# Loading rows of keys and rearranging the opening of an attention + two-MLP kernel

## The chip, the cores and the metric

The kernel runs on one NeuronCore of a Trainium2 chip. The metric is device time in microseconds (us), from launch to end. The kernel before takes 1071.01 us (median of three runs, 1069.24 to 1071.11). Its engines have one instruction queue each: PE (TensorE, the matmuls; PEld is its weight load), DVE (VectorE), ACT (ScalarE), POOL (GpSimd), and SP, which here only issues DMAs. An instruction waits at the head of its queue for semaphores, and everything behind it waits with it.

## The reference

Chunked attention over 4 batches, 8 heads, 768 positions of width 64: each chunk of 32 queries sees 8 memory keys and a window of the sequence. Two MLPs of width 512 to 2048 to 512 follow, over 3072 tokens.

```python
for c in range(nc):                      # 24 chunks of 32 queries
    l_start, r_end = max(0, c*32 - 16), min(S, c*32 + 32 + 8)
    k_full = concat([mem_k, k[:, :, l_start:r_end]])      # 8 + up to 56 keys
    scores = scale * q_c @ k_full.T
    a = exp(scores - max(scores)); a = a / (sum(a) + 1e-9)
    out[chunk] = a @ concat([mem_v, v[:, :, l_start:r_end]])
x = out as 3072 x 512
h = x @ w_in;  x = (h - tanh(h)) @ w_out                  # first MLP
h = x @ w2_in; x = g2(h) @ w2_out                         # second MLP, g2 = clipped (h+1)^2/4
```

The weights come as 64-bit words. The kernel reads them as pairs of 32-bit integers and turns each pair into a float by a few integer operations ("rounding" below).

## The kernel before, in words

**Attention by groups.** Four chunks (128 queries, all heads) make a group; there are 24 groups, and four groups make a block of 512 tokens. For one group `att_scores` runs 64 small matmuls (64x32 by 64x64) into PSUM, `att_max` takes the maxima and subtracts them (DVE), `att_exp` is one ACT instruction, `att_sum` adds and inverts (DVE), `att_transpose` turns the weights by four PE matmuls against an identity, `att_at` copies them out (ACT), `att_values` runs 64 small matmuls, `att_norm` divides (DVE), `att_x` transposes the result (PE), `att_xh` and `att_xl` write it as a rounded part (ACT) and a rest (DVE): `xh`, `xl`, the input of the first MLP.

**The input.** The host lays out, for each chunk, its queries, 128 keys (`KEYS`: 8 of memory and 120 of the sequence, for each of four head pairs) and the values. A chunk needs only the first 64 of these keys (`WIN`): the memory and 56 of the sequence. Before, each chunk's 64 keys are a DMA of their own, 128 partitions by four runs of 64 floats (`att_keys`, line 364).

**The opening** is what the change touches: the first four groups, with a queue order written by hand (no scheduler moves anything). Their loads are issued on SP group by group: queries, four key windows, a weight slice `w_in` (from the second group on), four loads of values; then the fourth weight slice. Then come the loads of group 4, and the weight slices 4, 5, 6 and 7, each into one of four `stage` buffers, which is free when the POOL addition of the slice before in it is done. While the groups run, PE is given extra matmuls on zeros (`warm`, `fill`). Before, each of groups 0 to 2 has ten of them, in three places.

**Weight slices.** Slice i is rounded in five instructions after its load: two on ACT (`round_act`, lines 138 and 141), two on DVE (`round_mag`, 147 and 148), one on DVE (`round_sign`, 156) and an integer addition on POOL (161). Then ACT makes its rounded part `whi` (173) and DVE the rest `wlo` (180). The first MLP's first product, `hidden(s)`, takes slice s: `whi` by `xh`, `whi` by `xl`, `wlo` by `xh`, four matmuls each, into a PSUM tile `h`; then `gate` applies tanh and the subtraction. Its first step, `hidden(0)`, is run early for the 384 tokens of groups 0 to 2, in between the work of group 3, and for the last 128 tokens after group 3.

After the opening the kernel interleaves the `hidden` and `output` products of the first MLP with the attention of the later groups, then runs the second MLP, up to the end at about 1070 us.

Of the kernel before, what the change touches and what calls it, by code (L numbers as in the profile page):

```python
# [8 lines left out]
F32 = mybir.dt.float32  # L9
# [18 lines left out]
KEYS = NMEM + CTX  # L28
WIN = NMEM + LEFT + CHUNK + SEEN
NPAIR = H // 2  # L30
KC = DM // 128
FC = DFF // 128
NEG = -3.0e38

GC = 4
# [7 lines left out]


WARM = 11
KEEP = {"s": 6, "t": 2, "v": 2}

LAG = FC

# [29 lines left out]
def tile_memory_attention_two_mlps(  # L79
# [25 lines left out]
    def slot(tag, name, dtype=F32):  # L105
        return slots.tile([128, 512], dtype, tag=tag, name=name)
# [13 lines left out]
    def load_weights(phase, which, fc, tag=None):  # L120
        src = ((w1_in, w1_out), (w2_in, w2_out))[phase][which]
        if tag is None:
            tag = f"stage{loaded[0] % STAGES}"
            loaded[0] += 1
        stage = wide.tile([128, 512, 2], I32, tag=tag, name=f"stage{phase}{which}_{fc}")
        nc.sync.dma_start(out=stage, in_=src[fc])
        stage_t[phase, which, fc] = stage
# [25 lines left out]
    def round_sign(phase, which, fc):  # L153
        stage = stage_t.pop((phase, which, fc))
        bits = raw_t[phase, which, fc].bitcast(I32)
        nc.vector.scalar_tensor_tensor(
            out=bits, in0=stage[:, :, 1], scalar=-0x40000000, in1=bits, op0=ALU.bitwise_and, op1=ALU.bitwise_or
        )

        eng = nc.vector if phase else nc.gpsimd  # L160
        eng.tensor_tensor(out=bits, in0=bits, in1=stage[:, :, 0], op=ALU.add)  # L161
# [14 lines left out]
    def split_weights_lo(s, which):  # L176
        phase, b, fc = steps[s]
        r, hi = raw_t[phase, which, fc], split_t[s, which]
        lo = slot(f"wlo{which}_{s % (W1O if which else 2)}", f"wlo{which}_{s}", F32R)
        nc.vector.tensor_tensor(out=lo, in0=r, in1=hi.bitcast(F32), op=ALU.subtract)  # L180
        split_t[s, which] = hi, lo
# [162 lines left out]
    def att_load_start(t, values):  # L344
        if not free:
            free.extend(slot(f"g{i}", f"start{i}") for i in range(FC))
            free.extend(slot(f"y{i}", f"starty{i}") for i in range(KC))
        q, k0, k1, v0, v1 = free[5 * t:5 * t + 5]
        if values:
            att_v(t, (v0, v1))  # L350
        else:
            att_keys(t, q, (k0, k1))

    def att_keys(t, q, k):
        q = q.rearrange("p (j a c) -> p j a c", j=GC, a=NPAIR)
        k = [x.rearrange("p (j a c) -> p j a c", j=2, a=NPAIR) for x in k]
        src = qkv[t * GC:(t + 1) * GC]
        nc.sync.dma_start(
            out=q.rearrange("p j a c -> p j (a c)"),
            in_=src[:, :, :NPAIR * TQ].rearrange("j p c -> p j c"),  # L360
        )
        ks = src[:, :, NPAIR * TQ:QK].rearrange("j p (a c) -> j p a c", a=NPAIR)
        for j in range(GC):
            nc.sync.dma_start(out=k[j // 2][:, j % 2], in_=ks[j, :, :, :WIN])  # L364
        st[t] = {
            "q": [q[:, j] for j in range(GC)],
            "k": [k[j // 2][:, j % 2] for j in range(GC)],
        }

    def att_v(t, v):  # L370
        v = [x.rearrange("p (j c) -> p j c", j=2) for x in v]
        src = qkv[t * GC:(t + 1) * GC]

        for i in range(2):
            for u in range(2):
                c = QK + u * 4 * D
                nc.sync.dma_start(
                    out=v[i][u * WIN:(u + 1) * WIN],
                    in_=src[2 * i:2 * i + 2, :WIN, c:c + 4 * D].rearrange("j p c -> p j c"),
                )  # L380
        st[t]["v"] = [v[j // 2][:, j % 2] for j in range(GC)]
# [5 lines left out]
    def att_scores(t, pair):  # L387
        qt, kt = st[t]["q"], st[t]["k"]
        sp = pair[:, :, 4 * D:].rearrange("p c (a k) -> p c a k", a=NPAIR)
        for pr in range(NPAIR):  # L390
            for j in range(GC):
                for hh in range(2):
                    nc.tensor.matmul(  # L393
                        sp[j * CHUNK:(j + 1) * CHUNK, hh, pr, :],
                        qt[j][hh * D:(hh + 1) * D, pr, :],
                        kt[j][hh * D:(hh + 1) * D, pr, :],
                        start=True, stop=True,
                    )
        st[t]["sp"] = sp

    def att_max(t):

        e = slots.tile([128, 4, 2, WIN], F32, tag=f"e{t % 2}", name=f"e{t}")
        mx = att.tile([128, 2, NPAIR], F32, tag="mx", name=f"mx{t}")
        s = st[t]["sp"]

        if t % GPB == 0:
            nc.vector.memset(s[:CHUNK, :, :, NMEM:NMEM + LEFT], NEG)
        if t % GPB == GPB - 1:
            nc.vector.memset(s[128 - CHUNK:, :, :, WIN - SEEN:], NEG)  # L410
        nc.vector.tensor_reduce(out=mx, in_=s, op=ALU.max, axis=AX.X)
        st[t]["e"] = e
        if t in BY_HEAD:
            nc.vector.tensor_scalar(out=mx, in0=mx, scalar1=-scale, scalar2=None, op0=ALU.mult)
            st[t]["mx"] = mx
            return
        for hh in range(2):
            nc.vector.tensor_tensor(
                out=e.rearrange("p (b c) u k -> p c u b k", c=2)[:, hh],
                in0=s[:, hh].rearrange("p (u b) k -> p u b k", u=2),  # L420
                in1=mx[:, hh].rearrange("p (u b) -> p u b", u=2)[:, :, :, None].to_broadcast([128, 2, 2, WIN]),
                op=ALU.subtract,
            )
# [71 lines left out]
    def att_xl(t):  # L495
        b, o = t // PER, t % PER * GQ
        xh, xl = x_tiles(0, b)
        nc.vector.tensor_tensor(  # L498
            out=xl[:, :, o:o + GQ], in0=st.pop(t)["xp"], in1=xh[:, :, o:o + GQ].bitcast(F32), op=ALU.subtract
        )  # L500
# [52 lines left out]
    def hidden(s, n0=0, n1=N, parts=range(3)):  # L553
        phase, b, fc = steps[s]
        xh, xl = x_tiles(phase, b)
        hi, lo = split_t[s, 0]
        if s not in h_t:
            h_t[s] = ps_h.tile([128, 512], F32, tag="h", name=f"h{s}")[:, :N]
        hp = h_t[s][:, n0:n1]
        for j in parts:  # L560
            w, x = ((hi, xh), (hi, xl), (lo, xh))[j]
            for kc in range(KC):
                nc.tensor.matmul(  # L563
                    hp, w[:, kc * 128:(kc + 1) * 128], x[:, kc, n0:n1],
                    start=j == 0 and kc == 0, stop=j == 2 and kc == KC - 1,
                )
# [471 lines left out]
    def warm(n, ps):  # L1038
        for _ in range(n):
            nc.tensor.matmul(ps, zeros[:, :128], zeros, start=True, stop=True)  # L1040
# [3 lines left out]
    warm(WARM, fill)  # L1044
    for j in range(PER):
        att_load_start(j, False)
        if j:
            load_weights(0, 0, j - 1)
        att_load_start(j, True)
    load_weights(0, 0, PER - 1)  # L1050
    att_load(PER)

    def start_scores(j):
        pool, tag = ((ps_a, "a"), (ps_acc, "acc0"))[j % 2]
        st_pair[j] = pool.tile([128, 2, 512], F32, tag=tag, name=f"start_a{j}")
        att_scores(j, st_pair[j])

    start_scores(0)
    for j in range(PER):
        last = j == PER - 1  # L1060
        if not last:
            warm(KEEP["s"], fill)
        att_max(j)
        if j:
            att_xl(j - 1)
        if last:
            split_weights_lo(0, 0)
            hidden(0, 0, EARLY_N, (0,))
        if 1 < j:
            round_sign(0, 0, j - 2)  # L1070
        att_exp(j)
        att_sum(j)
        tx = ps_acc.tile([128, 2, 512], F32, tag="acc1", name=f"start_tx{j}")
        att_transpose(j, tx[:, 0, :])
        att_at(j)
        if j == 2:
            split_weights_hi(0, 0)
        if j:
            round_act(0, 0, j - 1)
        if last:  # L1080
            split_weights_hi(1, 0)
            hidden(0, 0, EARLY_N, (1,))
        else:
            warm(KEEP["t"], fill)
        att_values(j, st_pair.pop(j))
        if last:
            hidden(0, 0, EARLY_N, (2,))
        else:
            warm(KEEP["v"], fill)
            start_scores(j + 1)  # L1090
        att_norm(j)
        if last:
            split_weights_lo(1, 0)
        if j:
            round_mag(0, 0, j - 1)
        att_x(j, tx[:, 1, :])
        att_xh(j)
    att_xl(PER - 1)
    round_sign(0, 0, 2)
    round_act(0, 0, 3)  # L1100
    round_rest(0, 0, 3)
    for j in range(AHEAD):
# [105 lines left out]
```

## Time and profile before

| | |
|---|---|
| runs | 1071.01, 1071.11, 1069.24 us |
| profiled execution: span, first to last instruction | 1070.1 us |
| what lies around the span (median of the runs less the span) | 0.9 us |
| PE busy | 1052.4 us (98%), 7589 matmuls |
| DVE, ACT, POOL busy | 855.7, 650.0, 42.7 us |
| bytes by DMA | 259.37 MB, mean 242 GB/s |
| chain that ended last, by engine | PE 93%, DMA 2%, SP queue 2%, ACT 1%, DVE 1% |

The share of PE says little by itself: in the opening it counts the matmuls on zeros. So the stages have to be read apart: the first 55 us, in which PE stops and waits, and the rest, in which it hardly does. In the rows of the trace, the time at a row's start is counted from the span's start, and the bracket at its end says how long the engine had stood idle before it and what ended that.

### The profile page before, as it was taken

How to read it: one execution, taken by the hardware profiler on the slowest of the kernel's cores; microseconds unless marked ns; L12 is line 12 of the kernel's file. 1: busy time of each engine (PE TensorE's matmuls, PEld its weight loads, DVE VectorE, ACT ScalarE, POOL GpSimd, SP SyncE). 2: the span in 40 equal slices, each digit the busy share in tenths (PEclk: the TensorE clock that was granted, in tenths of full speed). 3: DMA queues.
4: the chain of work that ended last, by engine and by line, in shares of the span. 5: the costliest groups of instructions: out<-in, count | busy, mean ns of one | idle time of the engine just before them, and what ended most of it. 6: DMA issues, size and time to landing. Idle time of an engine off the chain costs nothing.

```text
span 1070.1 us, 21112 instructions
## 1 busy us (share of the span) xinstructions
PE 1052.4 (98%) x7589; PEld 859.7 (80%) x7589; DVE 855.7 (80%) x1511; ACT 650.0 (61%) x1203; POOL 42.7 (4%) x38
## 2 busy tenths in 40 slices
PE   7799999999999999999999999999999999999998
PEld 3577888888888888888888888888888888888887
DVE  4898987877799999999999778698477787476854
ACT  2687756555455565565566677757477666577553
POOL 0232212000000000000000000000000000000000
PEclk9999999999999999999999999999999999999999
DMA  8999887898889999876487978787766877766774
GB/s 207 245 258 247 260 240 207 258 292 272 266 269 315 325 302 292 292 261 205 154 278 263 313 221 259 210 277 214 232 194 195 261 224 232 214 194 195 203 203 146
DMA packets 212088, 259.37 MB, mean 242 GB/s; under 512 B 65424, under 2 KB 129168, under 8 KB 211984
## 3 DMA queue, kind: packets, MB, share of 16 engines
q1 hardware_dynamic: 211840, 257.88, 80.2%
q8 instruction: 61, 1.00, 0.4%
q14 instruction: 43, 0.35, 0.1%
q10 hardware_dynamic: 144, 0.13, 0.0%
HBM read 199.23 MB, written 58.72 MB: 241 GB/s over the span
## 4 chain that ended last, share of the span: by engine, by line
PE 93%; DMA 2%; SPq 2%; ACT 1%; DVE 1%; issue 0%; ACTq 0%
PE h L563 23%; PE acc L893 21%; PE acc L601 17%; PE qa L805 12%; PE qc L805 6%; PE qb L805 3%; PE acc_-1_1_7132 L893 2%; PE acc_-1_0_7131 L893 2%; DMA stage<-w_in 2%; PE a L467 1%; SPq L364 1%; PE a L393 1%; PE acc_-1_1_7508 L893 1%; PE acc_-1_0_7507 L893 1%; PE b L487 1%; PE b L453 1%
## 5 line engine op out<-in xcount | busy, mean ns | idle before, releaser
L893 PE MATMUL acc<-ghi,inG 128*128 128x512 f32 x672 | 183.0, 389 | 0.0
L576 ACT ACTIVATE g<-h 128x512 f32<-128x512 f32 x96 | 57.7, 601 | 176.7 <-PE h L563 154.9
L893 PEld LDWEIGHTS acc<-ghi,inG 128*128 128x128 f32 x672 | 126.2, 188 | 26.1
L227 DVE TENSOR_TENSOR glo<-g,ghi 128x512 fp32r<-128x512 f32 x174 | 117.8, 688 | 27.4 <-ACT ghi L226 26.3
L805 PE MATMUL qa<-xc,inP 128*128 128x512 f32 x576 | 139.3, 389 | 0.0
L226 ACT ACTIVATE ghi<-g 128x512 fp32r<-128x512 f32 x174 | 107.3, 627 | 43.6 <-DVE glo L227 21.1
L805 PEld LDWEIGHTS qa<-xc,inP 128*128 128x128 f32 x576 | 108.1, 188 | 22.4
L563 PE MATMUL h<-xh,whi 128*128 128x512 f32 (+2 forms) x388 | 105.6, 394 | 3.9 <-DVE g L577 1.9
L893 PE MATMUL acc<-glo,inG 128*128 128x512 f32 x336 | 107.0, 389 | 0.1
L563 PE MATMUL h<-xl,whi 128*128 128x512 f32 (+2 forms) x388 | 104.0, 390 | 0.1
L563 PE MATMUL h<-xh,wlo 128*128 128x512 f32 (+2 forms) x388 | 103.8, 389 | 0.0
L577 DVE TENSOR_TENSOR g<-h,g 128x512 f32<-128x512 f32 x96 | 66.0, 688 | 38.7 <-ACT g L576 38.1
L563 PEld LDWEIGHTS h<-xh,whi 128*128 128x128 f32 x388 | 71.5, 188 | 21.2 <-issue 4.1
L743 ACT ACTIVATE t<-g,half 128x512 f32<-128x512 f32 x72 | 52.2, 725 | 59.1 <-DVE g L739 59.1
L563 PEld LDWEIGHTS h<-xl,whi 128*128 128x128 f32 x388 | 73.0, 189 | 15.2 <-DVE xl L498 0.2
L563 PEld LDWEIGHTS h<-xh,wlo 128*128 128x128 f32 x388 | 72.1, 188 | 14.7
L180 DVE TENSOR_TENSOR wlo<-raw,whi 128x512 fp32r<-128x512 f32 x112 | 80.7, 720 | 0.0
L173 ACT ACTIVATE whi<-raw 128x512 fp32r<-128x512 f32 x112 | 70.5, 630 | 6.5 <-POOL raw L161 6.5
L601 PE MATMUL acc<-ghi,whi 128*128 128x512 f32 x256 | 74.0, 403 | 0.0
L893 PEld LDWEIGHTS acc<-glo,inG 128*128 128x128 f32 x336 | 63.0, 188 | 13.5 <-DVE glo L227 0.5
L805 PE MATMUL qc<-xc,inP 128*128 128x512 f32 x288 | 73.1, 389 | 0.0
L601 PE MATMUL acc<-ghi,wlo 128*128 128x512 f32 x256 | 70.7, 390 | 0.0
(717 smaller groups left out, 1811.3 us busy)
## 6 DMA issues: line engine op xcount, KB each, us to landing
inP<-part SPq DMA_DIRECT2D x168, 256.0 KB, 3.0
inG<-part SPq DMA_DIRECT2D x168, 256.0 KB, 3.0
stage<-w_in SPq DMA_DIRECT2D x32, 512.0 KB, 6.0
stage<-w_out SPq DMA_DIRECT2D x32, 512.0 KB, 5.5
part<-preph SPq DMA_DIRECT2D x64, 256.0 KB, 4.6
whi<-w1o SPq DMA_DIRECT2D x48, 256.0 KB, 4.9
wlo<-w1o SPq DMA_DIRECT2D x48, 256.0 KB, 5.1
part<-prepl SPq DMA_DIRECT2D x48, 256.0 KB, 4.7
```

What stands on the lines that cost most here:

```text
L173: nc.scalar.activation(out=hi, in_=r, func=AF.Copy)
L180: nc.vector.tensor_tensor(out=lo, in0=r, in1=hi.bitcast(F32), op=ALU.subtract)
L226: nc.scalar.activation(out=hi, in_=src, func=AF.Copy)
L227: nc.vector.tensor_tensor(out=lo, in0=src, in1=hi.bitcast(F32), op=ALU.subtract)
L364: nc.sync.dma_start(out=k[j // 2][:, j % 2], in_=ks[j, :, :, :WIN])
L563: nc.tensor.matmul(hp, w[:, kc * 128:(kc + 1) * 128], x[:, kc, n0:n1], start=j == 0 and kc == 0, stop=j == 2 and kc == KC - 1,)
L576: nc.scalar.activation(out=g, in_=hp, func=AF.Tanh)
L577: nc.vector.tensor_tensor(out=g, in0=hp, in1=g, op=ALU.subtract)
L601: nc.tensor.matmul(acc_t[dm], w[:, dm * 128:(dm + 1) * 128], g, start=first and j == 0, stop=last and j == 2,)
L743: nc.scalar.activation(out=t, in_=h, func=AF.Relu, scale=0.5, bias=half)
L805: nc.tensor.matmul(o, w[:, k * 128:(k + 1) * 128], z[k], start=i in (1, 2, 5) and j == 0 and k == 0, stop=j == 2 and k == 1, skip_group_ch ...
L893: nc.tensor.matmul(bank[a][c], w[:, c * 128:(c + 1) * 128], g, start=first and j == 0, stop=last and j == 2, skip_group_check=True,)
```

## The change

In the first four groups the keys are no longer loaded window by window. A DMA brings a whole row of 128 keys (512 floats for each partition, in one run) for the chunks 0, 3, 6, 9, 12 and 15 (`REACH` is 3). The windows of these chunks are read from the row where it lies. For the other ten chunks POOL copies the 64 keys into a set of their own (`att_windows`): one copy for the 8 memory keys and one for the 56 others. The order of the opening changes too: the scores of group j + 1 stand directly behind the transposes of group j and ahead of its values; the slices' rounding is placed later; there are four matmuls on zeros for each of groups 0 to 2, in one place; and the third weight slice is loaded behind the fourth group's values.

```diff
+REACH = (KEYS - WIN) // CHUNK + 1
-KEEP = {"s": 6, "t": 2, "v": 2}
+KEEP = 4
...
+        for c in range(t * GC, (t + 1) * GC):
+            if c % REACH == 0:
+                k = free.pop(0)
+                nc.sync.dma_start(out=k, in_=qkv[c, :, NPAIR * TQ:QK])
+                k_rows.append(k.rearrange("p (a c) -> p a c", a=NPAIR))
...
+    def att_windows(t):
+        keys = []
+        for c in range(t * GC, (t + 1) * GC):
+            m, u = divmod(c, REACH)
...
+            if u:
+                w = k_win[m][:, u - 1]
+                nc.gpsimd.tensor_copy(out=w[:, :, :NMEM], in_=k_rows[m][:, :, :NMEM])
+                nc.gpsimd.tensor_copy(
+                    out=w[:, :, NMEM:], in_=k_rows[m][:, :, NMEM + u * CHUNK:NMEM + u * CHUNK + WIN - NMEM]
+                )
+                keys.append(w)
+            else:
+                keys.append(k_rows[m][:, :, :WIN])
...
-        if j:
+        if 0 < j < PER - 1:
             load_weights(0, 0, j - 1)
         att_load_start(j, True)
-    load_weights(0, 0, PER - 1)
+    for j in range(PER - 2, PER):
+        load_weights(0, 0, j)
...
     for j in range(PER):
         last = j == PER - 1
+        att_transpose(j, start_tx[:, 0, :])
         if not last:
+            att_windows(j + 1)
+            att_scores(j + 1, start_a[(j + 1) % 2])
+        att_at(j)
+        att_sum(j)
         if last:
+            split_weights_hi(0, 0)
+            round_mag(0, 0, 1)
             split_weights_lo(0, 0)
+            hidden(0, 0, EARLY_N, (0, 1))
+            round_sign(0, 0, 1)
         else:
+            att_max(j + 1)
+        att_values(j, start_a[j % 2])
         if last:
             hidden(0, 0, EARLY_N, (2,))
         else:
+            att_exp(j + 1)
+            warm(KEEP, fill)
         att_norm(j)
+        if j == 2:
+            round_mag(0, 0, 0)
+        att_x(j, start_tx[:, 1, :])
         att_xh(j)
+        if 0 < j:
+            round_act(0, 0, j - 1)
+        att_xl(j)
+        if j == 2:
+            round_sign(0, 0, 0)
+    split_weights_hi(1, 0)
+    split_weights_lo(1, 0)
+    round_rest(0, 0, 2)
     round_act(0, 0, 3)
     round_rest(0, 0, 3)
```

The order on SP at the loads of the fourth group. `start` and `starty` are the places of queries, keys and values, `stage` those of the weight slices. Before:

```order
L358 DMA start_161<-qkv_t 128x4x128
L364 DMA starty_162<-qkv_t 128x4x64 x2
L364 DMA starty_163<-qkv_t 128x4x64 x2
L126 DMA stage_2_202<-w_in 128x1024
L377 DMA starty_164<-qkv_t 64x2x256 x2
L377 DMA starty_165<-qkv_t 64x2x256 x2
L126 DMA stage_3_208<-w_in 128x1024
```

And now:

```order
L354 DMA start_159<-qkv_t 128x4x128
L361 DMA start_160<-qkv_t 128x512
L361 DMA start_161<-qkv_t 128x512
L407 DMA starty_162<-qkv_t 64x2x256 x2
L407 DMA starty_163<-qkv_t 64x2x256 x2
L128 DMA stage_2_196<-w_in 128x1024
L128 DMA stage_3_198<-w_in 128x1024
```

Two rows of 512 floats stand for four windows, and the third slice (`stage_2`) stands behind the values.

The order on PE from the last scores of the fourth group to its values (`start_a`: scores and values, `xn` to `start_tx`: `att_x` of the third group, `e` to `start_tx`: transposes of the fourth, `h`: `hidden(0)`). Before:

```order
L393 MATMUL start_a_529<-starty_163,start_161 32x64 x4
L487 MATMUL start_tx_481<-ident,xn_562 128x128 x4
L563 MATMUL h_579<-xh_354,whi_0_488 128x384 x4
L453 MATMUL start_tx_591<-ident,e_571 128x128 x4
L563 MATMUL h_579<-xl_355,whi_0_488 128x384 x4
L467 MATMUL start_a_529<-starty_164,at_596 32x64 x4
```

And now (the third group's values and the matmuls on zeros stand between the scores and the first row here):

```order
L517 MATMUL start_tx<-ident,xn_553 128x128 x4
L483 MATMUL start_tx<-ident,e_511 128x128 x4
L593 MATMUL h_584<-xh_357,whi_0_578 128x384 x4
L593 MATMUL h_584<-xl_358,whi_0_578 128x384 x4
L497 MATMUL start_a_213<-starty_162,at_572 32x64 x4
```

Both early parts of `hidden(0)` now stand together, directly ahead of the fourth group's values.

The order on ACT around the fourth group's `att_xh` (`xh`), with the rounding of the slices (`raw`, `stage`) and their rounded parts (`whi`). Before:

```order
L138 ACTIVATE raw_2_598<-stage_2_202 128x512
L141 ACTIVATE stage_2_202<-stage_2_202 128x512
L173 ACTIVATE whi_1_601<-raw_1_490 128x512
L493 ACTIVATE xh_354<-start_tx_591 128x4x128
L138 ACTIVATE raw_3_657<-stage_3_208 128x512
```

And now:

```order
L488 ACTIVATE at_572<-start_tx 128x512
L175 ACTIVATE whi_0_578<-raw_0_459 128x512
L523 ACTIVATE xh_357<-start_tx 128x4x128
L140 ACTIVATE raw_2_638<-stage_2_196 128x512
L143 ACTIVATE stage_2_196<-stage_2_196 128x512
L175 ACTIVATE whi_1_642<-raw_1_562 128x512
L140 ACTIVATE raw_3_650<-stage_3_198 128x512
```

The rounding of slice 2 and the rounded part of slice 1 have moved from ahead of `xh` to behind it; the rounded part of slice 0 now stands directly ahead of it.

## Rows read from the trace of the kernel before

**Rows 1.** The chain that ended last, 0 to 112 us: start, us, what.
```profile
39.99 4.93 DMA stage<-w_in
...
45.65 0.44 DVE raw L147
...
54.81 2.98 PE h L563 x12
```

**Rows 2.** Stretches: us, busy by engine (instructions), granted clock, DMA share, GB/s.
```profile
33.00:36.50 3.50, 2.81 (x48) 2.13 (x50) 2.38 (x5) 2.23 (x4) 1.30 (x1) 0.65 1.11 263
54.74:110.00 55.26, 54.19 (x794) 42.72 (x789) 50.64 (x96) 45.15 (x130) 16.14 (x13) 1.00 1.01 254
210.00:1070.00 860.00, 856.26 (x5086) 707.13 (x5084) 684.24 (x1190) 520.14 (x910) 0.00 (x0) 1.00 0.79 243
```

**Rows 3.** DMA view, 0 to 45 us.
```profile
DMA packets 16916, 9.70 MB, mean 216 GB/s; under 512 B 11043, under 2 KB 16163, under 8 KB 16911
...
q1 hardware_dynamic: 16911, 9.62, 87.1%
```

**Rows 4.** DMA view, 900 to 1000 us.
```profile
DMA packets 11151, 20.36 MB, mean 204 GB/s; under 512 B 1242, under 2 KB 1242, under 8 KB 11145
...
q1 hardware_dynamic: 11145, 20.29, 71.8%
```

**Rows 5.** PE in order of time, 18 to 40 us: start, us, instruction, idle before.
```profile
18.93 1.06 PE L453 MATMUL start_tx<-ident,e 128*128 128x128 f32 x4
...
20.78 1.18 PE L467 MATMUL start_a<-start,at 64*32 64x64 f32 x64
...
27.06 0.86 PE L467 MATMUL start_a<-start,at 64*32 64x64 f32 x64 [0.32 <-ACT at L458]
...
29.68 0.76 PE L393 MATMUL start_a<-starty,start 64*32 64x64 f32 x52 [0.43 <-DMA starty<-qkv_t]
...
31.71 1.37 PE L563 MATMUL h<-xh,whi 128*128 128x384 f32 x4 [0.69 <-ACT xh L493]
...
33.58 1.63 PE L563 MATMUL h<-xl,whi 128*128 128x384 f32 x4
...
36.98 0.98 PE L563 MATMUL h<-xh,wlo 128*128 128x384 f32 x4
37.83 0.66 PE L487 MATMUL start_tx<-ident,xn 128*128 128x128 f32 x4
39.18 0.66 PE L563 MATMUL h<-xh,whi 128*128 128x128 f32 x4 [0.69 <-ACT xh L493]
```

**Rows 6.** DVE in order of time, 25 to 46 us.
```profile
25.39 0.68 DVE L156 SCALAR_TENSOR_TENSOR raw<-stage,raw 128x512 int32<-128x512 int32 x1
...
26.70 0.83 DVE L446 TENSOR_SCALAR r<-r 128x8 f32<-128x8 f32 x1
...
30.47 0.69 DVE L411 TENSOR_REDUCE mx<-start_a 128x8 f32<-128x512 f32 x1 [0.82 <-PE start_a L393]
31.20 0.76 DVE L418 TENSOR_TENSOR e<-start_a,mx 128x256 f32<-128x256 f32 x2
...
37.09 0.69 DVE L477 TENSOR_TENSOR xn<-start_a,r 128x512 f32<-128x512 f32 x1 [1.64 <-PE start_a L467]
...
38.29 0.42 DVE L147 TENSOR_SCALAR raw<-raw 128x512 f32<-128x512 f32 x1
...
39.16 0.69 DVE L498 TENSOR_TENSOR xl<-start_tx,xh 128x512 fp32r<-128x512 f32 x1
```

**Rows 7.** ACT in order of time, 27 to 39 us.
```profile
27.54 0.63 ACT L173 ACTIVATE whi<-raw 128x512 fp32r<-128x512 f32 x1 [0.53 <-POOL raw L161]
...
34.52 0.67 ACT L138 ACTIVATE raw<-stage 128x512 f32<-128x512 f32 x1
35.08 0.65 ACT L141 ACTIVATE stage<-stage 128x512 int32<-128x512 uint32 x1
...
38.53 0.60 ACT L493 ACTIVATE xh<-start_tx 128x512 fp32r<-128x512 f32 x1 [2.28 <-PE start_tx L487]
```

**Rows 8.** POOL in order of time, 0 to 28 us.
```profile
0.73 0.20 POOL masks.py:197 MEMSET ident<- 128x128 f32 x1 [0.29 <-POOLq L1196]
...
26.22 1.29 POOL L161 TENSOR_TENSOR raw<-raw,stage 128x512 int32<-128x512 int32 x1 [24.91 <-DMA starty<-qkv_t]
```

More of the change, by code (lines that the diff above doesn't have):

```diff
@@ L347, in att_load_start @@
             free.extend(slot(f"y{i}", f"starty{i}") for i in range(KC))
-        q, k0, k1, v0, v1 = free[5 * t:5 * t + 5]
         if values:
-            att_v(t, (v0, v1))
-        else:
-            att_keys(t, q, (k0, k1))
+            att_v(t, (free.pop(0), free.pop(0)))
+            return
+        q = free.pop(0).rearrange("p (j a c) -> p j a c", j=GC, a=NPAIR)
+        nc.sync.dma_start(
+            out=q.rearrange("p j a c -> p j (a c)"),
+            in_=qkv[t * GC:(t + 1) * GC, :, :NPAIR * TQ].rearrange("j p c -> p j c"),
+        )
[4 more added lines that the diff above has]
+                k_rows.append(k.rearrange("p (a c) -> p a c", a=NPAIR))
+        st[t] = {"q": [q[:, j] for j in range(GC)]}
+    k_rows, k_win = [], []
+    def att_windows(t):
+        keys = []
+        for c in range(t * GC, (t + 1) * GC):
+            m, u = divmod(c, REACH)
+            if len(k_win) <= m:
+                k_win.append(slot(f"prep{m}", f"startk{m}").rearrange("p (u a c) -> p u a c", u=2, a=NPAIR))
+            if u:
[3 more added lines that the diff above has]
+                    out=w[:, :, NMEM:], in_=k_rows[m][:, :, NMEM + u * CHUNK:NMEM + u * CHUNK + WIN - NMEM]
+                )
+                keys.append(w)
+            else:
+                keys.append(k_rows[m][:, :, :WIN])
+        st[t]["k"] = keys
     def att_keys(t, q, k):
@@ L1046, in tile_memory_attention_two_mlps @@
         att_load_start(j, False)
-        if j:
+        if 0 < j < PER - 1:
             load_weights(0, 0, j - 1)
         att_load_start(j, True)
-    load_weights(0, 0, PER - 1)
+    for j in range(PER - 2, PER):
+        load_weights(0, 0, j)
     att_load(PER)
[L1053 to L1058, printed above, removed]
+    start_a = [pool.tile([128, 2, 512], F32, tag=tag, name=f"start_a{i}") for i, (pool, tag) in enumerate(((ps_a, "a"), (ps_acc, "acc0")))]
+    start_tx = ps_acc.tile([128, 2, 512], F32, tag="acc1", name="start_tx")
+    att_windows(0)
+    att_scores(0, start_a[0])
+    att_max(0)
+    att_exp(0)
     for j in range(PER):
         last = j == PER - 1
+        att_transpose(j, start_tx[:, 0, :])
         if not last:
[L1062 to L1065, printed above, removed]
+            att_windows(j + 1)
+            att_scores(j + 1, start_a[(j + 1) % 2])
+        att_at(j)
+        att_sum(j)
         if last:
+            split_weights_hi(0, 0)
+            round_mag(0, 0, 1)
             split_weights_lo(0, 0)
[L1068 to L1082, printed above, removed]
-        else:
-            warm(KEEP["t"], fill)
-        att_values(j, st_pair.pop(j))
+            hidden(0, 0, EARLY_N, (0, 1))
+            round_sign(0, 0, 1)
+        else:
+            att_max(j + 1)
+        att_values(j, start_a[j % 2])
         if last:
@@ L1088, in tile_memory_attention_two_mlps @@
         else:
-            warm(KEEP["v"], fill)
-            start_scores(j + 1)
+            att_exp(j + 1)
+            warm(KEEP, fill)
         att_norm(j)
[L1092 to L1096, printed above, removed]
-        att_xh(j)
-    att_xl(PER - 1)
-    round_sign(0, 0, 2)
+        if j == 2:
+            round_mag(0, 0, 0)
+        att_x(j, start_tx[:, 1, :])
+        att_xh(j)
+        if 0 < j:
[6 more added lines that the diff above has]
+    round_rest(0, 0, 2)
     round_act(0, 0, 3)
```

## The prediction, made before the changed kernel was run

> **What bounds the kernel now.** I read the stretches first. From 210 us on PE is busy for 856.26 of 860 us, and from 54.74 to 110 for 54.19 of 55.26 [rows 2]: there is no time to win there, and whatever the opening gains or loses until 54.74 is carried to the end as it is. So the question is when PE begins the run of `hidden` products that starts at 54.81 [rows 1].
>
> Then I followed the chain back from there. It runs through ACT and DVE work to the rounding of weight slice 4 (DVE, 45.65), and that waits for the slice's load, issued at 39.99 and landed 4.93 later [rows 1]. So before, the opening is set by the DMA queue. From 45.65 to 54.8 the chain is engine work without a wait for DMA; I keep these 9.1 us as they are and ask only when DVE can begin the rounding of slice 4 in the changed kernel.
>
> **Part 1: the loads.** Up to 45 us the queue moved 9.62 MB with the 16 engines busy for 87.1%, that is 39.2 us of work [rows 3]. Late in the kernel nearly all packets are of 2 KB, and 20.29 MB took 71.8 us of work, so 283 GB/s [rows 4]. The 20 key DMAs of the first stretch (16, and four of group 4) have 512 packets of 256 B each, 2.62 MB of the 9.62. The other 7.0 MB at 283 GB/s are 24.7 us, which leaves 14.5 us for the keys, 0.72 us each. A row of keys is 256 KB in 2 KB packets: 0.93 us. So 16 x 0.72 - 6 x 0.93 = 5.9 us of DMA work go. If bytes alone counted it would be less: 0.52 MB at 216 GB/s, 2.4 us.
>
> When does that help? Before, the last keys of the fourth group arrive at 29.68 [rows 5]. Ahead of them stand all queries, keys, the values of three groups and two slices; in the new order it is the same list. So the last row (call its landing T) comes at 29.7 - 5.9 = 23.8, or at 27.3 by bytes alone. I take 24.3, near the first, because there the engines' own busy time is counted; half a microsecond is added since the last load is twice as large.
>
> The DMA page of the Trainium skill ("DMA: Bandwidth & Descriptors", Specifications) wants at least 512 B per transfer for full rate and says that smaller ones are read, modified and written. The trace agrees in direction [rows 3, 4]: per byte the 256 B packets come out at 1.5 times the price of 2 KB. At twice the price a key DMA would be 0.93 us by this estimate, T about 20.4, and the scores then wait for the group before, not for DMA, at about 23.
>
> **Part 2: the copies.** Two windows of the fourth group come from the row of chunk 12, which lands one row (0.93 us) before T. A window is two copies, 32 and 256 - 32 = 224 elements. The trace shows no POOL copy. Below: a POOL memset of 128 elements takes 0.20 us, so two instructions cost 0.4; above: the addition of 512 elements with two inputs takes 1.29 [rows 8]. I take 0.65 for a window, half of the addition, since there is half as much to move and one input. Two windows: 1.3 - 0.9 = 0.4 us behind T. The bounds are 0 and 1.7.
>
> **Part 3: the new order.** With the DMA earlier, a chain of engine work is late next. From T, with the durations shown [rows 5 to 8] and some 0.05 us for each handover:
> - windows and fourth scores, 0.4 + 0.86: T + 1.35
> - maxima 0.69 and subtraction 0.76: T + 2.85. The third group's division (0.69) now stands behind them on DVE: T + 3.5
> - `att_x` 0.66, `att_xh` 0.60, `att_xl` 0.69: T + 5.6. The sign step of slice 0 (0.68), before at 25.39, stands behind these: T + 6.25; POOL's addition 1.29: T + 7.6; `whi` of slice 0, 0.63: T + 8.25
> - PE waits here with both early parts of `hidden(0)`: 1.37 + 1.63 as shown [rows 5], T + 11.2. In that stretch the granted clock was 0.65, a mean of its levels of 1.2 and 2.4 GHz [rows 2]. The third part with the same 384 columns took 0.98 afterwards, so without the lower clock the two take 1.9: T + 10.2
> - queued behind them: the fourth values 0.86, division 0.69, `att_x` 0.66, `att_xh` 0.60: T + 14.15. That is 38.45 with T = 24.3, against 38.53 + 0.60 = 39.13 before [rows 7]: little is won by here
> - behind `xh` on ACT now both steps of slice 2 (1.2 [rows 7]) and `whi` of slice 1 (0.63): T + 15.9. On DVE `wlo` of slice 1 (0.7), the two magnitude steps (0.9, from 38.29 to 39.16 [rows 6]), the sign step (0.69), then POOL 1.29: T + 19.5
> - DVE's magnitude steps of slice 3 meet that addition. What then happens is to be seen in [rows 6, 8]: an 8-element step on DVE that began at 26.70 took 0.83 us and ended at 27.53, POOL's addition at 27.51. So: T + 20.4, sign T + 21.1, POOL T + 22.4; `wlo` of slice 2 waits for it and takes 0.6 on DVE; the rounding of slice 4 begins at T + 23.0.
>
> Slice 4 itself is not late: its load stands behind 5.9 us less of DMA work (about 39 us against 44.9), and its `stage` buffer is free at T + 7.6.
>
> With T = 24.3 this is 47.3 at the lower clock and 46.3 at the full one, against 45.65: 1.65 or 0.65 later, in the middle 1.15. What was a wait for DMA has become a longer chain through one slice after another.
>
> Priced at nothing: the ten windows of groups 0 to 2 and the copies (POOL is idle until 26.22 [rows 8]; their rows land while the group before computes, and if they did not, a group's start would move by the 0.65 of a window); 18 fewer matmuls on zeros (their place is a wait; what they could cost is the clock, a rival below). Slices 6 and 7 can be loaded only after POOL's additions for slices 2 and 3, here at T + 19.5 and T + 22.4, about 44 and 46.7 against some 42 and 44.4. I count nothing for that, because the queue is emptier then; if it is not, it costs up to 2 us more.
>
> **The sum.** Span 1070.1 + 1.15 = 1071.25, and 0.9 around it as in the runs shown: 1072.1 us, against the median of 1071.01. Own range: T from 23.8 (-0.5) to 25.3 (+1.0), the clock 0.5 either way, the windows -0.4 to +1.3: 1070.1 to 1074.
>
> **The rivals.**
> *Faster: the saved DMA time comes through.* T is 23.0 (a key DMA costs 0.77 us rather than 0.72, which the split of the 9.62 MB doesn't exclude), the clock stays full, and DVE's steps for slice 3 are not held by POOL, so they begin at T + 18.2 rather than 19.5 and `wlo` does not wait either (together 1.6). The rounding of slice 4 begins at 23 + 22.0 - 1.6 = 43.4, 2.3 us sooner than before: 1068.7. For it: before, the opening really waited for DMA, and 5.9 us of that work go. Against it: the step at 26.70 shows the hold [rows 6].
>
> *Slower: the lower clock.* Place: PE between T and T + 14. There are 12 matmuls on zeros where there were 30, and the granted clock had already fallen to 0.65 with 30 [rows 2]. Price: transposes take 1.06 rather than 0.66, the 64 small matmuls 1.18 rather than 0.86 [rows 5]. On the chain stand scores and values (0.64), two `att_x` (0.8), the third part of `hidden(0)` and its wait (0.3), and the half microsecond that I split above: 2.2 us, 1074.3. It decides if the granted clock is down for most of 24 to 38 us.
>
> *The change does not do what it says:* the landing goes by bytes, T = 27.3, 3 us later than assumed: 1075.1. For it: before, the rate was 216 to 263 GB/s whatever was moved [rows 2, 3].
>
> **How the numbers follow.** This measurement can tell 0.2% (2.1 us) from no change, so 1068.9 and 1073.1 are the marks. My forecast has 0.51 (0.43 within the marks, 0.08 above), the faster rival 0.22 (0.18 below the mark, 0.04 within), the lower clock 0.20 (0.17 above, 0.03 within), the bytes 0.07, all above. Faster 0.18, same 0.50, slower 0.32. The range of 8 in 10 goes from the faster rival to a little above the lower clock: 1068.6 to 1074.8.
>
> **What the profile after would show.** Part 1: the fourth scores begin at 24 to 26 us rather than 29.7. Part 2: a pair of copies on POOL takes 0.4 to 1.3 us. Part 3: PE idle for about 3 us ahead of `hidden(0)`, ended by ACT's `whi`, at about 32.5; `xh` of the fourth group near 38.5; DVE's steps for slice 3 stretched to the end of a POOL addition; the chain between 24 and 45 us through DVE, ACT and POOL and no longer through a `stage` load. I am wrong if PE reaches its run of products before 52.5 or after 58, or if the wait that ends last there is still a DMA.

## The result, and the profile after

The changed kernel takes 1080.6 us (median of 4 runs, 1078.97 to 1081.34) against 1070.39 for the kernel before on the same chip: a ratio of 1.0088, 95% interval 1.0068 to 1.0109. It is some 10 us slower; 1072.1 was predicted. Its profiled execution has a span of 1079.5 us and took 1081.25.

Stretches of the changed kernel (columns as in [rows 2]):

```profile
20.00:30.00 10.00, 4.96 (x128) 3.42 (x127) 3.92 (x9) 2.94 (x5) 0.99 (x4) 0.66 0.88 246
30.00:40.00 10.00, 4.31 (x24) 2.59 (x25) 5.34 (x12) 3.57 (x6) 1.28 (x1) 0.66 0.30 68
40.00:50.00 10.00, 9.25 (x104) 7.58 (x103) 5.01 (x10) 3.83 (x7) 1.61 (x2) 0.82 0.29 102
54.74:110.00 55.26, 51.05 (x717) 39.85 (x716) 50.67 (x98) 45.03 (x142) 17.11 (x13) 1.00 0.98 257
210.00:1079.00 869.00, 864.88 (x5242) 714.18 (x5240) 691.10 (x1202) 522.79 (x915) 0.00 (x0) 1.00 0.79 243
```

From 20 to 40 us taken together PE, DVE and ACT are each idle for more than half of the time, and from 30 to 50 the DMA engines are idle for 70%: nothing is short, everybody waits. The run of products begins at 63.10 us where it began at 54.81 [rows 1]. Of the 9.4 us between the spans 8.3 are there by then.

The DMA view up to 45 us, against [rows 3]:

```profile
DMA packets 9321, 9.13 MB, mean 203 GB/s; under 512 B 2688, under 2 KB 7808, under 8 KB 9317
...
q1 hardware_dynamic: 9317, 9.07, 72.6%
```

and POOL at the fourth group, where it waits for the row of chunk 12:

```profile
22.95 0.21 POOL L375 COPY startk<-start 128x32 f32<-128x32 f32 x1 [6.45 <-DMA start<-qkv_t]
23.10 0.38 POOL L376 COPY startk<-start 128x224 f32<-128x224 f32 x1
23.42 0.21 POOL L375 COPY startk<-start 128x32 f32<-128x32 f32 x1
23.57 0.38 POOL L376 COPY startk<-start 128x224 f32<-128x224 f32 x1
```

So parts 1 and 2 came as forecast: the last row landed at 23.86 (T = 24.3 was forecast), a window's two copies come every 0.47 us (0.65 was taken). Yet the fourth scores began at 27.40. Why, PE shows in order of time (against [rows 5]; the idle time before an instruction and what ended it are in brackets):

```profile
17.35 0.66 PE L483 MATMUL start_tx<-ident,e 128*128 128x128 f32 x4 [1.41 <-DVE xl L528]
...
19.49 0.60 PE L1070 MATMUL fill<-zeros 128*128 128x512 bf16 x2
23.06 1.03 PE L1070 MATMUL fill<-zeros 128*128 128x512 bf16 x2 [2.96 <-issue]
...
28.27 1.07 PE L497 MATMUL start_a<-start,at 64*32 64x64 f32 x53
32.70 0.33 PE L497 MATMUL start_a<-start,at 64*32 64x64 f32 x11 [3.36 <-issue]
...
39.55 1.65 PE L593 MATMUL h<-xh,whi 128*128 128x384 f32 x4 [1.57 <-ACT whi L175]
```

Twice PE stops in the middle of a row of like instructions (after the second of four matmuls on zeros, after the 53rd of 64 value products) with no operand missing; "issue" says that it waited for nothing the profile shows. Counting all records of PE's queue (matmuls, weight loads and a handful of semaphore instructions), the stops are ahead of the 706th and the 962nd: 256 apart. The kernel before has one such stop, ahead of the 450th, again 256 earlier:

```profile
17.39 1.75 PE L1040 MATMUL fill<-zeros 128*128 128x512 bf16 x6 [2.74 <-issue]
```

The waits of PE from 10 to 66 us (total us, times, longest), before:

```profile
PE fill L1040 <- issue: 2.7, 1, 2.7
PE h L563 <- DVE g L577: 1.9, 1, 1.9
```

and after:

```profile
PE start_tx L483 <- DVE xl L528: 4.2, 3, 1.4
PE h L593 <- DVE g L607: 3.6, 2, 1.9
PE start_a L497 <- issue: 3.4, 1, 3.4
PE fill L1070 <- issue: 3.0, 1, 3.0
```

What PE waited for stands in the DMA view, in a queue of its own that loads instructions (q8; its 61 packets in the whole run are 15,616 instructions at 256 each, and PE has 15,658 records). Changed kernel, 15.8 to 20.4 us and then 20.4 to 21.6:

```profile
q1 hardware_dynamic: 1280, 1.21, 105.6%
```

```profile
q1 hardware_dynamic: 216, 0.20, 67.4%
q8 instruction: 1, 0.02, 5.7%
```

In these two stretches q8 moves nothing while PE runs through its block, and one packet (16,384 bytes, so 64 for each of 256 instructions) when PE has come to the end. That packet started at 20.47, took 1.08, and PE went on at 23.06; the other stop has a packet from 29.90 to 31.20 and goes on at 32.70; the one before had 14.61 to 15.89 and 17.39. PE resumed 1.50 to 1.51 us behind the packet each time. (The Trainium skill, "Advanced Engine Details and Errata", ISA Cache, gives a line of the instruction cache as 16 KB or 256 instructions. The packets agree with that; what filling a line costs does not stand there.)

The end of the block is not what starts the packet. In experiments 4 and 7 below the packets between 15 and 30 us start in mid-block, 1.9 to 4.0 us behind the border that PE passed last, and PE needs 6.0 us or more for a block. In the changed kernel PE was through the block it entered at 17.96 after 2.1 us, and its packet came 2.5 us behind the border; for the block entered at 23.06 PE needed 6.3 us, and the packet came 6.8 us behind. So PE stops where it gets through 256 instructions sooner than the next packet, begun after the border before, is there. This is read from the times; no run varied it by itself.

From the second stop on the order of the chain is the forecast one, only later. DVE at the rounding of slice 4, 45.65 before [rows 1]:

```profile
49.92 1.41 DVE L150 TENSOR_SCALAR raw<-raw 128x512 int32<-128x512 int32 x1
...
52.57 1.47 DVE L182 TENSOR_TENSOR wlo<-raw,whi 128x512 fp32r<-128x512 f32 x1
53.97 0.41 DVE L149 TENSOR_SCALAR raw<-raw 128x512 f32<-128x512 f32 x1
```

### The profile page after: what moved, and what is told of

It reads as the page before. It is cut to its first block, busy times and chain, and to the rows that moved or that the text cites. A ratio compares the mean times of both kernels' runs of the same rounds, so it can differ in the third digit from the quotient of the medians.

```text
span 1079.5 us, 21083 instructions
## 1 busy us (share of the span) xinstructions
PE 1052.2 (97%) x7571; PEld 860.8 (80%) x7571; DVE 855.9 (79%) x1511; ACT 649.7 (60%) x1203; POOL 47.6 (4%) x58
## 4 chain that ended last, share of the span: by engine, by line
PE 93%; ACT 3%; DVE 3%; issue 1%; DMA 0%; POOL 0%; SPq 0%; ACTq 0%
PE h L593 21%; PE acc L923 21%; PE acc L631 17%; PE qa L835 12%; PE qc L835 6%; PE qb L835 3%; PE acc_-1_1_7125 L923 2%; PE acc_-1_0_7124 L923 2%; PE a L497 1%; ACT e L465 1%; PE a L423 1%; PE acc_-1_1_7501 L923 1%; PE acc_-1_0_7500 L923 1%; PE b L517 1%; PE b L483 1%
## 5 line engine op out<-in xcount | busy, mean ns | idle before, releaser
L593 PE MATMUL h<-xh,whi 128*128 128x512 f32 (+2 forms) x388 | 105.6, 394 | 6.2 <-DVE g L607 3.6
L923 PEld LDWEIGHTS acc<-glo,inG 128*128 128x128 f32 x336 | 63.0, 188 | 13.5 <-DVE glo L229 0.5
```

The source lines that it names most:

```text
L593: nc.tensor.matmul(hp, w[:, kc * 128:(kc + 1) * 128], x[:, kc, n0:n1], start=j == 0 and kc == 0, stop=j == 2 and kc == KC - 1,)
L923: nc.tensor.matmul(bank[a][c], w[:, c * 128:(c + 1) * 128], g, start=first and j == 0, stop=last and j == 2, skip_group_check=True,)
```

## The experiments

Two causes are to be told apart: **A**, TensorE waits for its own instructions; **E**, the rounding of slices 0 to 3 has moved behind the third and fourth group and is late. Rivals: the rows or copies (B), the tile that transposes share with `att_xl` (C), the clock (D), an opening that does not hang on DMA at all (F). All times are medians; "before" is 1069.6 to 1070.0 in these sets.

**1. Rows alone.** The kernel before with the new `att_load_start` and `att_windows`, called in the old order:

```
 st_pair[j] = pool.tile(...)
+att_windows(j)
 att_scores(j, st_pair[j])
```

> Rows of keys and the windows that GpSimd copies, with the order of work and the place of the third slice as in the kernel before. Theory A (the ten microseconds come from TensorE waiting for its own instructions in the new order): the loads still end earlier, the order is the old one, so the run of products begins at 52 to 55 us against 54.8 before and the time is 1067 to 1071. Rival B (the copies, or the larger loads, are what costs): the run of products begins at 58 us or later and the time is 1075 or more.

1072.25 us, ratio 1.0020 (1.0007 to 1.0034). B falls: it is 8 us below the change. But it misses A's range too, and its runs spread from 1068.81 to 1075.03. PE has a stop of 3.7 us in the third scores, once more at a border (255 records behind the stop before it; single records can be missing):

```profile
PE start_a L423 <- issue: 3.7, 1, 3.7
PE fill L1070 <- issue: 2.8, 5, 2.1
```

**2. Order alone.** The changed kernel with the old `att_load_start`, without `att_windows`.

> The new order of work and the new place of the third slice, with each window loaded as before (20 small key loads, no copies). Theory A: two stalls of TensorE of about 3 us that end on nothing but its own instruction supply are seen again between 17 and 35 us, and the time is 1079 to 1085, at least that of the whole change. Rival B (the rows are at fault): about 1070.

1078.27, ratio 1.0078 (1.0063 to 1.0093). The loss is in the order, not in the rows. The stops are shorter than A said (1.64 and 0.72), the time a little below its range: 8.3 us are lost with 2.4 us of stops, a first sign that A isn't all.

**3. Free transposes.**

```
-att_transpose(j, start_tx[:, 0, :])
+att_transpose(j, fill)
```

> The changed kernel, with the transposes of the exponentials written into the tile of the matmuls on zeros, so that those of a group no longer wait for att_xl of the group before (three idle times of 1.41 us on TensorE). Theory C (this wait, met three times, is the loss): the run of products begins 3 to 4.5 us sooner, 1076 to 1077.5. Theory A: TensorE only reaches the end of its fetched instructions sooner and waits there the longer; the stalls grow to 4 us or more and the time stays at 1079 to 1081.

1078.83, ratio 1.0081 (1.0064 to 1.0098). The three waits for `xl` are gone (4.2 us), the time falls by 1.8, to just below A's range and well above C's. The second stop has grown to 4.5, as A said, but the first has shrunk to 0.80; the wait for `whi` of slice 0 has grown to 3.6:

```profile
PE start_a L497 <- issue: 4.5, 1, 4.5
PE h L593 <- DVE g L607: 3.6, 2, 1.9
PE h L593 <- ACT whi L175: 3.6, 1, 3.6
```

**4. Instruction shift.**

```
-warm(WARM, fill)
+for _ in range(64):
+    nc.tensor.matmul(fill[:, :88], zeros[:, :128], zeros[:, :88], start=True, stop=True)
```

> The changed kernel, with the 11 first matmuls on zeros of 512 columns replaced by 64 of 88 columns: the same 5632 columns in the same place, while TensorE waits for the first loads, but 106 instructions more. Everything behind stands 106 instructions later in TensorE's stream, so the borders of 256 instructions at which it stalled (the 706th and the 962nd) fall on other places, in the midst of the values of the second group and near the end of the scores of the fourth. Theory A: the stalls move to these places or go, at least one goes (it is asked for at 12 us rather than 18), and the time changes by 2 us or more, most likely to 1074 to 1078. Rivals C (the shared tile) and D (the lower clock): stalls at the same matmuls as in the changed kernel, and 1079.5 to 1081.5.

1076.70, ratio 1.0062 (1.0047 to 1.0077): 3.9 us below the change. In the profiled execution the two stops are gone but for 0.53, and DVE begins slice 4 6.5 us sooner than in the changed kernel:

```profile
PE h L593 <- DVE g L607: 3.6, 2, 1.9
...
PE fill L1070 <- issue: 0.8, 3, 0.3
PE start_a L497 <- issue: 0.7, 2, 0.5
```

```profile
47.43 0.41 DVE L149 TENSOR_SCALAR raw<-raw 128x512 f32<-128x512 f32 x1
```

The same waits for `xl` (4.2) are still there, so what was won is not C's. A is shown, for part of the loss.

**5. Rows and shift.** Experiment 1 with the cut of experiment 4.

> The rows and copies in the old order (as in the run of the rows alone), with the first 11 matmuls on zeros cut into 64 of the same columns, so that TensorE's borders of 256 instructions lie 106 instructions earlier. The run of the rows alone lost 3.72 us at such a border at 20 us and its times spread over 6 us. Theory A (the saved DMA time was there and was eaten by the wait for instructions): no stall over 1.5 us ahead of 40 us and 1067 to 1069.5, below the kernel before. Rival F (DMA did not bound the opening in the end, VectorE does): 1069.5 to 1071 whatever the stalls do.

1068.70 (1067.26 to 1069.60), ratio 0.9993 (0.9984 to 1.0002). No stop above 1.07 us, 3.6 us below experiment 1, and the spread falls from 6.2 to 2.3 us: A's range. DVE begins slice 4 at 39.19, 6.5 us sooner than before; against the kernel before most of that doesn't show in the median, and the interval includes no change.

**6. Control.** The kernel before with the cut alone.

> The kernel before with the same cut of the first matmuls on zeros and nothing else: a control. It has one stall of 2.74 us at a border (at 14.65), which ends while the loads of the third group are still on their way. Theory A: the stall moves or goes, but the end hangs on a load at 45 us, so the time stays at 1069 to 1071. Rival (the cut itself is worth something, by the clock or by what it does to the first scores): a change of 2 us or more.

1072.32, ratio 1.0023 (1.0012 to 1.0034). The stop is gone, as A allowed, but the time is 2.7 us above before: that is the rival's mark of 2 us or more, as a loss. The cut is not free. Its profiled execution has the lower clock on the first products behind the fourth group, where before had 1.00:

```profile
40.00:45.00 5.00, 5.00 (x17) 4.23 (x17) 4.71 (x6) 2.20 (x4) 2.64 (x2) 0.50 0.96 309
```

So what experiments 4 and 5 gained isn't a gift of the cut itself. That the stop of 2.7 us could go without a gain agrees with its having been hidden before.

**7. Early rounding.** Experiment 4, with the steps of slices 0 to 3 put between those of the groups and taken out of their old places:

```
 att_at(j)
+if 1 < j: split_weights_hi(j - 2, 0)
 att_sum(j)
+if j: round_mag(0, 0, j - 1)
...
 att_norm(j)
+if j: round_sign(0, 0, j - 1)
 att_x(j, start_tx[:, 1, :])
 att_xh(j)
+round_act(0, 0, j)
 att_xl(j)
+if 1 < j: split_weights_lo(j - 2, 0)
```

> The changed kernel with the cut first matmuls and with slices 0 to 3 rounded as early as they have landed, each step between the steps of the groups, rather than behind the third and fourth group. Without it (the run with the cut alone) the queue stood from 36 to 47 us, since the loads of slices 4 to 7 wait for buffers that GpSimd's additions free, and 35 to 50 us moved 2.01 MB against 3.73 before. Theory E (what is left of the loss is this late rounding): rounding of slice 4 begins at 40 to 43 us against 47.43, over 3 MB are moved in 35 to 50 us, and the time is 1067 to 1071. Rival C (the order of scores and values, with the shared tile of the transposes, is what is left): rounding of slice 4 at 46 us or later and 1075 to 1077, as with the cut alone.

1068.60 (1066.51 to 1069.83), ratio 0.9988 (0.9980 to 0.9997): 8.1 us below experiment 4, 12.0 below the change. The wait for `g` is gone, and DVE begins slice 4 at

```profile
39.57 0.41 DVE L149 TENSOR_SCALAR raw<-raw 128x512 f32<-128x512 f32 x1
```

E is shown. The order of scores and values, with the shared tile, is still in this kernel.

**8. Third slice.** The kernel before with `load_weights(0, 0, 2)` moved behind the fourth values.

> The kernel before, with only the load of the third weight slice moved behind the values of the fourth group. Theory (this part costs nothing by itself): the fourth group's keys land about 2 us sooner and slice 2 later, 1069 to 1071. Rival (slice 2 is late and holds the chain of the slices): 1072 to 1074.

1070.77, ratio 1.0013 (1.0004 to 1.0022). This part costs about a microsecond, within the theory's range.

**9. Early rounding alone.** Experiment 7 with `warm(WARM, fill)` as in the change.

> The changed kernel with slices 0 to 3 rounded as early as in the run with early rounding, but with the first 11 matmuls on zeros whole again, so that the borders of 256 instructions lie where they lay in the changed kernel. If the two losses stand side by side (wait for instructions, late rounding), this takes the second alone: 1080.6 - 8.1 = 1072.5, between 1071 and 1075, with one or two stalls of TensorE of about 3 us between 19 and 35 us. If the early rounding alone is the whole answer: 1067.5 to 1069.5. If the stalls alone are: 1076 or more.

1074.44 (1071.17 to 1077.10), ratio 1.0033 (1.0019 to 1.0047). The two losses do stand side by side: both stops are back, and a spread of 6 us with them:

```profile
PE start_a L497 <- issue: 2.8, 1, 2.8
PE fill L1070 <- issue: 2.5, 1, 2.5
```

With this the four cases are complete:

| median, us | late rounding | early rounding |
|---|---|---|
| borders as in the change | 1080.6 | 1074.4 |
| borders 106 instructions earlier | 1076.7 | 1068.6 |

The shift is worth 3.9 and 5.8 (and 3.6 in the old order, experiment 5 against 1), the early rounding 6.2 and 8.1; together 12.0. Part of either goes by way of the clock, see experiment 12.

**10. Two more buffers.** Experiment 4, slices 4 and 5 loaded into free tiles:

```
 for j in range(AHEAD):
+    if j < 2: stage = xsp.tile(..., tag=f"x{'hl'[j]}1")  # viewed as [128, 512, 2], then loaded
+    else:
     load_weights(0, 0, PER + j)
```

> The changed kernel with the cut first matmuls, the rounding late as in the change, and slices 4 and 5 loaded into the buffers of the second x, which are free at that time, so that the queue needn't wait for GpSimd's additions and goes on to the loads of the next groups. Theory E1 (the late rounding costs through the queue that stands from 36 to 47 us): over 1.5 MB are moved in 36 to 47 us, the loads behind come sooner, and the time is 2 us or more below the 1076.7 of the cut alone. Theory E2 (it costs through the chain of VectorE, ScalarE and GpSimd steps itself, which would begin the rounding of slice 4 at 47.4 all the same): 1075.5 to 1077.5.

1075.03 (1073.20 to 1076.18), ratio 1.0043 (1.0029 to 1.0057). DMA from 36 to 47 us, first in experiment 4, then here:

```profile
DMA packets 266, 1.02 MB, mean 92 GB/s; under 512 B 21, under 2 KB 21, under 8 KB 265
```

```profile
DMA packets 3724, 3.16 MB, mean 287 GB/s; under 512 B 2255, under 2 KB 3275, under 8 KB 3723
```

Three times the data, and slice 4 starts no sooner (47.91 here, 47.43 there):

```profile
47.91 0.41 DVE L149 TENSOR_SCALAR raw<-raw 128x512 f32<-128x512 f32 x1
```

The time is 1.7 below experiment 4, with ranges that overlap: between the two, short of E1's 2 us and 0.5 below E2's range, though the profiled execution has a stop of 1.5 us at 13.97 that experiment 4's has not. The beginning of slice 4 is as E2 said. The standing queue is at most a smaller part of the 8.1 us that the late rounding costs.

**11. Early rounding and free transposes.** Experiments 7 and 3 together.

> The run with early rounding and cut first matmuls, with the transposes of the exponentials in the tile of the matmuls on zeros, so that they don't wait for att_xl (1.41 us three times in that run). Theory C (this wait is on the chain once nothing else is late): the run of products begins 2 to 4 us sooner and 1065 to 1067.5. Theory A and F (TensorE then only waits for instructions, or the groups wait for VectorE or their loads): 1068 to 1070.

1067.07 (1066.24 to 1068.67), ratio 0.9973 (0.9961 to 0.9984). The best version: 2.9 us below the kernel before and 13.5 below the change. That is C's range and 1.5 us below experiment 7, but the intervals of the two overlap, and DVE begins slice 4 only 0.5 us sooner (39.06), where C asked for 2 to 4: that the wait of 1.41 us counts once nothing else is late is likely, not shown.

**12. No matmuls on zeros between the groups.** Experiment 7 with `KEEP = 0`.

> The run with early rounding and cut first matmuls, without the 12 matmuls on zeros between the groups. Theory D (the granted clock is what the fewer matmuls on zeros cost): the clock stays at its lower level through most of 10 to 45 us and the time is 1070 or more. Rival (they stand on TensorE ahead of att_x and cost 0.5 to 1 us a group): 1066 to 1068.5.

1070.85, ratio 1.0009 (1.0000 to 1.0018), 2.3 us above experiment 7. Experiment 7 from 20 to 30 us, then this one:

```profile
20.00:30.00 10.00, 6.12 (x172) 3.85 (x160) 7.98 (x18) 5.61 (x10) 3.55 (x6) 0.90 0.99 273
```

```profile
20.00:30.00 10.00, 5.33 (x140) 3.96 (x140) 6.86 (x15) 4.73 (x9) 3.31 (x6) 0.50 1.08 272
```

D is real: with the granted clock at its lower level in this stretch (over 20 to 40 us 0.61 against 0.95 in experiment 7), the kernel is slower by about what the forecast's slower rival named (2.2). The stops bring some of this with them: experiment 9 has 0.58 from 20 to 40 us, about the clock of this run, and is 3.6 us above it. So of the 5.8 us that the shift is worth with early rounding, 2.3 go by way of the clock and 3.6 are the standing itself (an estimate from these three experiments; the 12 matmuls on zeros are gone in one of them). Experiment 4 has 0.74: of the 8.1 us of the early rounding an unknown part is clock too.

## Why the prediction was wrong

**What bounds the kernel: right.** What the opening lost until 54.8 came through: 8.3 us there, 9.4 at the end. My sign of being wrong came as well: PE reached its run of products at 63.10, after 58.

**Part 1 and part 2: right.** T was 23.86 against 24.3, a window 0.47 against 0.65. The estimate by the Trainium skill's page "DMA: Bandwidth & Descriptors" (T about 20.4, at a doubled price that I had assumed) was far off: the price of a key DMA that the rows gave is the one that held.

**Part 3: the step that failed is its first, "windows and fourth scores: T + 1.35", and with it "the third group's division: T + 3.5".** It lets PE run scores and values as soon as their operands are there. In the trace the fourth scores began 3.5 us behind T and the division at 33.11 us, 9.2 behind. The two stops, 6.3 us, are what held them: the first ends at 23.06, before T, but the third group's `att_x` and `xl` and the fourth scores' place on PE come behind it; the second stands in the third group's values, ahead of the division. The stop of the kernel before was among its waits (2.7 us, "issue") and I asked neither what it was nor where the next would fall; there it was hidden by loads that came later still (the fourth scores waited for their keys until 29.68 [rows 5]). With the loads as before and the new order (experiment 2) the stops are 1.64 and 0.72, with the rows 2.96 and 3.36: the groups run sooner into the borders, and the edit that saved DMA time is what made the stops long.

The other durations of part 3 were right, as experiment 4 shows, which has the same order without the stops (us; the forecast with T = 24.3, and in experiment 4 the last row lands at 24.30). Only PE's idle time ahead of `hidden(0)` was smaller than the 3 us named: 1.6, and 2.0 in experiment 4.

| end of | forecast | after | experiment 4 |
|---|---|---|---|
| sign step, slice 0 | 30.55 | 37.40 | 30.33 |
| `whi` of slice 0 | 32.55 | 39.50 | 32.43 |
| `xh` of the fourth group | 38.45 | 45.67 | 39.13 |
| POOL's addition, slice 2 | 43.8 | 51.05 | 44.51 |
| POOL's addition, slice 3 | 46.7 | 53.49 | 46.96 |
| beginning of slice 4 on DVE | 46.3 to 47.3 | 53.97 | 47.43 |

The hold of DVE by POOL that I read from one row came at both places named (1.41 and 1.47 us for steps of 0.43 and 0.69).

**The sum: one term left out, two too small.** Left out: the stops. By the profiled executions they are 6.5 us of the 8.3 in the opening (slice 4 on DVE at 53.97, in experiment 4 at 47.43); by the medians the shift is worth 3.9 of the 10.2. Too small: the longer chain. It was forecast at 1.15, the middle of 0.65 and 1.65; by the profiled executions it is 1.8 (47.43 in experiment 4 against 45.65 before), by the medians experiment 4 is still 6.7 us behind, and early rounding takes all of that back. The other one too small is "0.9 around it": the profiled execution after has 1081.25 - 1079.5 = 1.75, and those of the experiments 1.8 to 2.1. With 1.75 the profiled execution of before would be one of about 1071.8 (an estimate), well above its median, so that differences between spans come out some 2 us too small for the medians. The profiled executions of experiments 4 and 5 are besides 1.1 and 1.4 us under their own medians. Together this accounts for experiment 4 being 3.7 us behind by the spans and 6.7 by the medians, and for 0.9 being left of the 4.9 us that experiment 5 saves by the spans. So in the medians the late rounding weighs more than the stops, though a pair of traces alone says the opposite. My own range of 1070.1 to 1074 was besides not what its terms give: added to 1072.1 they run from 1070.7 to 1074.9.

**The rivals.** *Lower clock:* its condition came true (a granted clock of 0.62 from 24 to 38 us, 0.88 before), and by experiment 12 it is worth 2 to 3 us. But experiment 4 has 0.63 there and is 3.9 us faster: it is at most a part of the loss. *Bytes:* refuted by T. *Faster:* the saved DMA time does come through in the opening where neither stops nor late rounding stand in the way, in experiments 5 and 7 (slice 4 on DVE at 39.19 and 39.57); in the medians 0.9 and 1.0 us of it are left, the first not clear of no change. I gave that rival a chance, but for the order as changed, in which rounding was late by itself. That the rounding's chain was the new bound I had said; that it alone would cost 6 to 8 us in the medians I had not.

**What stays open.** Why a packet starts 2 to 4 us behind a border in some places and 6.8 in another. In the changed kernel q1 had the engines full until the packet came (105.6% above), which suggests that it queues behind the loads; but in experiment 4 q1 was as full from 19.1 to 21.5 us (111.1%), and its packet started 2.4 us behind the border. No run held the loads back with the same instructions. Why the cut costs the kernel before 2 us and more beyond the one profile with the lower clock. And 1 to 2 us that come and go between 195 and 440 us and at the last store, mostly with PE busy; in experiment 7 1.3 us of them are one more stop at a border, at 225 us.

## What to carry to other kernels

A wait that ends on "issue" in the midst of like instructions is a cost with a place: count the engine's instructions, find the spacing (256 here), and ask where the borders fall in the new order, above all where hundreds of small matmuls stand back to back (here PE was through a block in 2.1 us). A stop that is hidden today can be one to be paid once its cover is removed. And steps that feed a later stage should be put as early as their data allow, not where the code reads best: moved from behind the groups to between them, the rounding gave back 6 to 8 us.

## What was not expected of the hardware

- TensorE takes its instructions in blocks of 256 by DMA packets of 16 KB, which took 0.96 to 1.37 us in the openings where PE waited for them; it resumed 1.34 to 1.58 us after the packet's end in all eight such stops of 2 us and more here.
- Some kernels spread over 6 us from run to run. In experiment 9 that goes with the granted clock of the run: 1071.17 us at 0.997, 1075.2 to 1077.1 at 0.987 to 0.989. In experiment 1 it does not (1068.81 at 0.998, 1075.03 at 0.997). Nor do stops make it: the changed kernel with two spreads over 2.4 us in four runs, experiment 6 with none in its profile over 5.7 in eleven.
- 64 matmuls on zeros instead of 11, with the same columns in all, made the kernel before 0.23% slower (experiment 6).
